# Moving 32 of 128 rows of each value tile from TensorE to GpSimd and VectorE, with wider matmuls around them

## The chip, the core and the metric

The kernel runs on one core of one Trainium2 chip. The metric is the device time of one execution in microseconds, lower is better. Each time is the median of several runs. The profile is one execution on the same chip, recorded by the hardware; its span goes from the first to the last instruction.

## The reference

One decode step for 4 sequences with one token each: a modulation from `c`, attention with 32 heads over a cache of 4096 positions, and a feed-forward block. All in float32.

```
x = A_x                                              # [4, 1, 512]
mod = (silu(c) @ w_mod).reshape(4, 6, 1, 512)        # w_mod [512, 3072]
sa, ca, ga, sb, cb, gb = mod[:, 0], ..., mod[:, 5]
h = layernorm(x) * (1 + ca) + sa
q = (h @ wq).reshape(4, 1, 32, 128).transpose(0, 2, 1, 3)
scores = einsum("bhqd,bhkd->bhqk", q, k_cache) * 128 ** -0.5   # k_cache, v_cache [4, 32, 4096, 128]
o = einsum("bhqk,bhkd->bhqd", softmax(scores), v_cache)
x = x + ga * (o.transpose(0, 2, 1, 3).reshape(4, 1, 4096) @ wo)
h = layernorm(x) * (1 + cb) + sb
x = x + gb * (silu(h @ w1) @ w2)                     # w1 [512, 1792], w2 [1792, 512]
```

The caches are 537 MB of the 567 MB that are read.

## The kernel before

**Tiles.** The work on the caches is cut into N = 32 steps, n = 4t + b: four heads (t = 0 to 7) of one sequence (b = 0 to 3). A step's keys are one tile `k` of 128 partitions x 128 rows x 128 elements, 8.39 MB; partition p holds 128 successive positions of head p // 32 of the four. The values `v` are laid out alike. Three slots of this size (pool `kv`) hold in turn wm, wq, k(0), v(0), k(1), v(1), ... and last the weights wo, and w1 with w2. SP issues all their loads (`fetch`, L82), in order, each when the tile before it in its slot has been read for the last time: k(n+1) goes where v(n-1) was, v(n+1) where k(n) was, wo where v(30) was, w1 and w2 where k(31) was.

**A step.** `make_qb` spreads the query of the step's four heads over the partitions by a matmul (`qb` in PSUM) and copies it to SBUF (`qw`). `mult` multiplies the keys by it in place (L252): GpSimd the first NA = 56 rows, VectorE the other 72. `red` (L257, VectorE) sums each row to a score in `sc` [128, 128]: first the 72 rows, later the 56. `rowmax`, `bmax` (a transpose on TensorE) and `negmax` make the head's maximum; `softexp` takes the exponential (ScalarE), and then GpSimd spreads the result into `pz`, two block-diagonal operands for TensorE, each for half of the rows. `pv` (L297) then multiplies with the values: 32 matmuls, each with 32 columns of `pz` and four value rows (512 elements), spread over four groups of TensorE's columns, and summed in PSUM (`po`) over two steps.

**Every two steps** `gather` picks from `po` what belongs together (VectorE, L308) and adds it by four matmuls into `od` (L314); every four steps `norm` and `spread` divide by the sums and turn the result into the operand `oz`.

**The end.** Step 31 loads and multiplies its keys in two halves, so that its first half can begin earlier; of each half GpSimd takes 28 rows, VectorE 36. After the last `pv` come `project` (L346, with wo, for t = 0 to 3, then 4 to 6, then 7), the last `gather` and `spread` between them, the residual (L415), the second layernorm, and the feed-forward block: up (L424), SiLU by tanh (L166 and L167, ScalarE and VectorE), a transpose (L170), down (L434), the last residual (L438, L439) and the output DMAs. `busy` issues matmuls with no use for their result.

**Order.** The schedule is written out by hand: every engine executes its instructions in the order of the program's text, and waits come from the data and the buffers alone. So the order in the loop body is the order on each engine:

Of the kernel before, what the change touches and what calls it, by code (L numbers as in the profile page):

```python
# [17 lines left out]
def kernel(  # L18
# [32 lines left out]
    NA = 56  # L51
    SCALE = 1.0 / math.sqrt(Dh)
# [54 lines left out]
    tmp = s0.take(P)  # L107
    csT, hT = s0.take(NK, W), s0.take(NK, W)
# [50 lines left out]
    for t in pz:  # L159
        nc.gpsimd.memset(t, 0.0)  # L160
    oz = const.tile([P, NT, R, B], F32, name="oz")
# [15 lines left out]
    def mods(dsts, i):  # L177
        p = psum([P, 4, P], "q", 2)
        for u in range(len(dsts)):
            for k in range(NK):  # L180
                for g in range(G):
                    o = (i + u) * D + g * P
                    nc.tensor.matmul(  # L183
                        p[W * g : W * (g + 1), u, :], csT[:, k, :], wmt[:, k, o : o + P],
                        start=k == 0, stop=k == NK - 1,
                    )
        for u, d in enumerate(dsts):
            nc.scalar.activation(
                d, p[:, u, :], AF.Copy,
                scale=0.25 if i + u == 5 else 0.5, bias=1.0 if i + u in (1, 4) else 0.0,  # L190
            )
# [48 lines left out]
    def make_qb(n):  # L240
        m = work.tile([P, Dh], F32, tag="lnu", name=f"qm{n}", bufs=1)
        nc.scalar.activation(m, qn, AF.Copy, scale=sel[:, n : n + 1])  # L242
        p = psum([P, Dh], "q", 2)
        nc.tensor.matmul(p, blk.rearrange("p i x -> p (i x)"), m, start=True, stop=True)  # L244
        qb[n] = p
        qw[n] = work.tile([P, Dh], F32, tag="qw", name=f"qw{n}")
        nc.scalar.activation(qw[n], p, AF.Copy)  # L247
# [27 lines left out]
    def softexp(n):  # L275
# [4 lines left out]
        for h in range(2):  # L280
            nc.gpsimd.tensor_mul(  # L281
                pz[h][:, : HG * W].rearrange("p (g x) -> p g x", g=HG)[:, :, E:].rearrange("p g (i j) -> p g i j", i=HP),
                sc[n][:, HG * JJ * h : HG * JJ * (h + 1)].rearrange("p (g j) -> p g j", j=JJ)
                .unsqueeze(2).to_broadcast([P, HG, HP, JJ]),
                hm.unsqueeze(1).unsqueeze(3).to_broadcast([P, HG, HP, JJ]),
            )

    def pv(n):
# [4 lines left out]
        for j in range(NG):  # L293
# [7 lines left out]
                start=(a == 0 and j < G), stop=(a == 1 and j >= NG - G),  # L301
# [4 lines left out]
    def gather(t, q):  # L306
# [6 lines left out]
        for j in range(JJ):  # L313
            nc.tensor.matmul(  # L314
                od[t], spick[:, 2 - 2 * q : 2 - 2 * q + P], o[:, j, :],
                start=(q == 0 and j == 0), stop=(q == 1 and j == JJ - 1),
            )
# [21 lines left out]
    accp = psum([P, P], "acc", 1)  # L339
    nc.vector.memset(accp, 0.0)  # L340

    def project(lo, hi):
        for t in range(lo, hi):
            for r in range(R):
                for g in range(G):
                    nc.tensor.matmul(  # L346
                        accp[W * g : W * g + B, :], oz[:, t, r, :], wot[:, t, r, g * P : (g + 1) * P],
                        start=(t == 0 and r == 0), stop=(t == NT - 1 and r == R - 1),
                    )
# [3 lines left out]
    for n in range(N):  # L353
# [29 lines left out]
        red(n, 0, NA if n + 1 < N else NA // 2)  # L383
# [14 lines left out]
        if b == B - 1:  # L398
            norm(t)
        pv(n)  # L400
# [5 lines left out]

    idle = psum([P, P], "q", 2)
# [5 lines left out]
    x1, hg, y = (s2.take(P) for _ in range(3))  # L413
    h2T, hid, th, hidT = s2.take(NK, W), s2.take(FG), s2.take(FG), s2.take(NI, W)
# [53 lines left out]
```

## Time and profile before

| | us |
|---|---|
| time, median of 3 runs | 1323.45 (1323.39 to 1323.84) |
| the profiled execution: time | 1323.81 |
| the profiled execution: span | 1321.9 |
| TensorE busy (matmuls) | 398.0 |
| VectorE busy | 923.3 |
| GpSimd busy | 533.5 |
| ScalarE busy | 44.7 |
| mean granted TensorE clock | 0.636 of full |

In the profile PE is TensorE (PEld its weight loads), DVE VectorE, ACT ScalarE, POOL GpSimd, SP the engine that issues the loads. L252 is line 252 of the kernel. A float32 matmul leaves two records. The timeline's rows have the start and the duration in us, then engine, line, operation, the tiles written and read with partitions x elements, and in brackets how long the engine had been idle before and what released it.

### The profile page before, as it was taken

To read this page: it belongs to the slowest core of one execution; us is meant where nothing else is said; L and a number is where in the kernel's file an instruction comes from. 1 tells how busy PE (TensorE), PEld (TensorE's weight loads), DVE (VectorE), ACT (ScalarE), POOL (GpSimd) and SP (SyncE) were. 2 spreads that over 40 slices of the span, in tenths; PEclk is the share of its full clock that TensorE was granted. 3 is DMA by queue.
4 is the path that set the end of the run, shared out by engine and by line. 5 is a ranking of instruction groups with operands and counts; after the bars stand their busy time and mean duration, and the time that the engine had idled before them with its cause. 6 is when DMAs were issued, how large, how long until landed. Compare 5 with 4: busy or idle time off the path is not lost.

```text
span 1321.9 us, 7059 instructions
## 1 busy us (share of the span) xinstructions
PE 398.0 (30%) x2998; PEld 145.4 (11%) x2998; DVE 923.3 (70%) x335; ACT 44.7 (3%) x146; POOL 533.5 (40%) x111
## 2 busy tenths in 40 slices
PE   3321223323123333212333321323332132333146
PEld 2100001101010010101001010100100010010014
DVE  1267877766887666788667678776668876676971
ACT  1100000000000000000000000000000000000000
POOL 1234455433445533354543334454334445433540
PEclk9765566665566666566666656666655666665569
DMA  9999999999999999999999999999999999999998
GB/s 414 441 418 439 442 419 438 439 424 431 441 430 429 437 436 427 436 436 429 435 433 435 428 435 438 426 435 440 423 435 444 418 437 444 419 437 439 420 422 330
DMA packets 12287, 567.76 MB, mean 430 GB/s; under 512 B 1440, under 2 KB 1504, under 8 KB 2272
## 3 DMA queue, kind: packets, MB, share of 16 engines
q1 hardware_dynamic: 12048, 567.29, 99.4%
q8 instruction: 23, 0.38, 0.1%
q14 instruction: 8, 0.07, 0.0%
q0 software_dynamic: 128, 0.01, 0.0%
q10 hardware_dynamic: 80, 0.02, 0.0%
HBM read 567.30 MB, written 0.01 MB: 429 GB/s over the span
## 4 chain that ended last, share of the span: by engine, by line
DMA 32%; issue 31%; POOL 25%; PE 7%; DVE 4%; POOLq 0%; SPq 0%; DVEq 0%
DMA k<-in_A_k_cache_dram 26%; POOL k L252 24%; PE po L297 6%; DMA w<-in_B_w_dram 3%; DMA wq<-in_A_wq_dram 3%; DVE sc L257 3%; DVE k L252 1%; POOL pz L281 1%; PE q L221 1%; PE mx L231 0%; POOLq L281 0%; DVE o L308 0%; PE po L434 0%; PE mx L265 0%; SPq L123 0%
## 5 line engine op out<-in xcount | busy, mean ns | idle before, releaser
L252 POOL TENSOR_TENSOR k<-k,qw 128x7168 f32<-128x7168 f32 (+1 forms) x33 | 491.4, 14893 | 290.1 <-DMA k<-in_A_k_cache_dram 264.7
L257 DVE TENSOR_REDUCE sc<-k 128x72 f32<-128x9216 f32 (+2 forms) x66 | 554.4, 8422 | 1.1
L252 DVE TENSOR_TENSOR k<-k,q 128x9216 f32<-128x9216 f32 (+1 forms) x33 | 312.3, 9463 | 309.3 <-DMA k<-in_A_k_cache_dram 300.1
L297 PE MATMUL po<-v,pz 128*32 128x512 f32 x2048 | 292.1, 735 | 48.6 <-POOL pz L281 47.9
L281 POOL TENSOR_TENSOR pz<-sc,hm 128x256 f32<-128x256 f32 x64 | 37.9, 612 | 458.1 <-ACT sc L279 445.7
L265 PE MATMUL mx<-ident,rm 128*128 128x128 f32 x32 | 14.5, 453 | 531.2 <-DVE rm L261 531.2
L314 PE MATMUL od<-o,spick 128*128 128x128 f32 x128 | 32.3, 431 | 293.4 <-DVE o L308 293.4
L297 PEld LDWEIGHTS po<-v,pz 128*32 128x32 f32 x2048 | 71.2, 132 | 248.2 <-issue 191.9
L265 PEld LDWEIGHTS mx<-ident,rm 128*128 128x128 f32 x32 | 5.8, 181 | 538.8 <-issue 332.1
L314 PEld LDWEIGHTS od<-o,spick 128*128 128x128 f32 x128 | 27.7, 319 | 296.5 <-DVE o L308 296.3
L279 ACT ACTIVATE sc<-sc,nm 128x128 f32<-128x128 f32 x32 | 12.8, 401 | 891.9 <-DVE nm L273 891.9
L270 DVE TENSOR_REDUCE hx<-mx 128x4 f32<-128x128 f32 x32 | 9.3, 291 | 19.7 <-PE mx L265 19.7
L247 ACT ACTIVATE qw<-q 128x128 f32<-128x128 f32 x32 | 8.9, 277 | 302.9 <-PE q L244 302.9
L308 DVE TENSOR_TENSOR o<-po,jm 128x512 f32<-128x512 f32 x16 | 10.9, 680 | 8.4 <-PE po L297 8.4
L244 PE MATMUL q<-qm,blk 128*128 128x128 f32 x64 | 15.6, 326 | 1.5 <-ACT qm L242 1.5
L183 PE MATMUL q<-wm 128*32 128x128 f32 x192 | 9.2, 375 | 20.3 <-DVE wm L170 20.3
L244 PEld LDWEIGHTS q<-qm,blk 128*128 128x128 f32 x64 | 9.5, 188 | 27.0 <-issue 25.1
L242 ACT ACTIVATE qm<-qn,sel 128x128 f32<-128x128 f32 x32 | 12.4, 387 | 0.9 <-DMA xg<-in_A_x_dram 0.9
L221 PE MATMUL q<-wq,wm 128*32 128x512 f32 x64 | 9.3, 748 | 7.4 <-DMA wq<-in_A_wq_dram 7.4
L183 PEld LDWEIGHTS q<-wm 128*32 128x32 f32 x192 | 7.8, 153 | 21.0 <-DVE wm L170 20.3
L261 DVE TENSOR_REDUCE rm<-sc 128x1 f32<-128x128 f32 x32 | 9.1, 284 | 0.9
L167 DVE SCALAR_TENSOR_TENSOR wm<-wm 128x128 f32<-128x128 f32 x1 | 0.3, 291 | 12.3 <-ACT wm L166 12.3
(79 smaller groups left out, 104.2 us busy)
## 6 DMA issues: line engine op xcount, KB each, us to landing
k<-in_A_k_cache_dram SPq DMA_DIRECT2D x2, 4096.0 KB
wm<-in_w_mod_dram SPq DMA_DIRECT2D x1, 6144.0 KB
wo<-in_A_wo_dram SPq DMA_DIRECT2D x1, 4096.0 KB
wo<-in_A_wo_dram SPq DMA_DIRECT2D x1, 2048.0 KB
wo<-in_A_wo_dram SPq DMA_DIRECT2D x2, 1024.0 KB, 35.2
w<-in_B_w_dram SPq DMA_DIRECT2D x2, 1024.0 KB
w<-in_B_w_dram SPq DMA_DIRECT2D x1, 1792.0 KB
w<-in_B_w_dram SPq DMA_DIRECT2D x2, 896.0 KB
```

The lines of the kernel that those rows point to most:

```text
L183: nc.tensor.matmul(p[W * g : W * (g + 1), u, :], csT[:, k, :], wmt[:, k, o : o + P], start=k == 0, stop=k == NK - 1,)
L221: nc.tensor.matmul(pq[i][W * g : W * (g + 1), :], hT[:, k, :], wqt[:, k, ch * CW : (ch + 1) * CW], start=k == 0, stop=k == NK - 1,)
L242: nc.scalar.activation(m, qn, AF.Copy, scale=sel[:, n : n + 1])
L244: nc.tensor.matmul(p, blk.rearrange("p i x -> p (i x)"), m, start=True, stop=True)
L252: eng.tensor_mul(kt[n][:, lo:hi, :], kt[n][:, lo:hi, :], src[n].unsqueeze(1).to_broadcast([P, hi - lo, Dh]))
L257: nc.vector.tensor_reduce(sc[n][:, lo:hi], kt[n][:, lo:hi, :], axis=AX.X, op=ALU.add)
L265: nc.tensor.transpose(p, nm[n].to_broadcast([P, P]), ident)
L279: nc.scalar.activation(sc[n], sc[n], AF.Exp, bias=nm[n], accum_out=rs[t][:, b : b + 1])
L281: nc.gpsimd.tensor_mul(pz[h][:, : HG * W].rearrange("p (g x) -> p g x", g=HG)[:, :, E:].rearrange("p g (i j) -> p g i j", i=HP), sc[n][:, ...
L297: nc.tensor.matmul(po[t, q][W * g : W * (g + 1), :], pz[h][:, o : o + W], vt[n][:, JJ * j : JJ * (j + 1), :].rearrange("p j d -> p (j d)") ...
L308: nc.vector.tensor_mul(o, po[t, q].rearrange("p (j d) -> p j d", j=JJ), jm.unsqueeze(2).to_broadcast([P, JJ, Dh]))
L314: nc.tensor.matmul(od[t], spick[:, 2 - 2 * q : 2 - 2 * q + P], o[:, j, :], start=(q == 0 and j == 0), stop=(q == 1 and j == JJ - 1),)
```

## The change

- `vmult` (new): after `pz`, GpSimd multiplies the first NV = 32 rows of v(n) in place by their weights, for all steps but the last. `first(n)` is 8 (NV // JJ) there, and 0 in the last step.
- `vsum` (new): in the next step, behind VectorE's product with k(n+1) and ahead of its reductions, VectorE sums these 32 rows (the 32 elements of one sum lie 128 elements apart), and one matmul with `hs` adds the sum to `po`.
- `pv` leaves these rows out: 24 matmuls for 32; `pz` has half as many elements for the first operand.
- In the last step GpSimd takes 36 of each half's 64 rows (NL = 72) for 28, VectorE 28 for 36. Both of GpSimd's halves are reduced last.
- `make_qb` makes the queries of four steps with one 512-wide matmul.
- `gather`: VectorE first adds the four parts (a strided reduction), one matmul for four.
- `project`: 512-wide matmuls, a quarter as many; the parts then stand in four groups of partitions and are added by the matmuls `xa` from a copy `ac`.
- `mods`: 512-wide matmuls too, then four products and matmuls to bring the parts in place.
- A tanh on one column, ahead of the feed-forward block.

```diff
+    NL = 72
+    NV = 32
...
+    hs = const.tile([P, W + E], F32, name="hs")
+    nc.vector.memset(hs, 0.0)
+    nc.vector.tensor_copy(hs[:, E : 2 * E].rearrange("p (i j) -> p i j", i=HP)[:, :, 0], hm)
...
     def mods(dsts, i):
...
+        for k in range(NK):
+            for u in range(n):
+                nc.tensor.matmul(
+                    p[W * u : W * (u + 1), :], csT[:, k, :], wmt[:, k, (i + u) * D : (i + u + 1) * D],
+                    start=k == 0, stop=k == NK - 1,
+                )
...
+        for g in range(G):
+            m = mm[:r, g % 2, :n, :]
+            nc.vector.tensor_mul(
+                m, p[:r, g * P : (g + 1) * P].unsqueeze(1).to_broadcast([r, n, P]),
+                hm[:r, :n].unsqueeze(2).to_broadcast([r, n, P]),
+            )
+            nc.tensor.matmul(z[W * g : W * (g + 1), :, :], sel[:r, :], m, start=True, stop=True)
...
     def make_qb(n):
-        m = work.tile([P, Dh], F32, tag="lnu", name=f"qm{n}", bufs=1)
-        nc.scalar.activation(m, qn, AF.Copy, scale=sel[:, n : n + 1])
-        p = psum([P, Dh], "q", 2)
-        nc.tensor.matmul(p, blk.rearrange("p i x -> p (i x)"), m, start=True, stop=True)
-        qb[n] = p
+        if n % B == 0:
+            m = work.tile([P, B, Dh], F32, tag="o", name=f"qm{n}", bufs=1)
+            for b in range(B):
+                nc.scalar.activation(m[:, b, :], qn, AF.Copy, scale=sel[:, n + b : n + b + 1])
+            p = psum([P, B, Dh], "q", 2)
+            nc.tensor.matmul(p, blk.rearrange("p i x -> p (i x)"), m, start=True, stop=True)
+            for b in range(B):
+                qb[n + b] = p[:, b, :]
...
+    def first(n):
+        return NV // JJ if n < N - 1 else 0
+
+    def vmult(n):
+        if first(n):
+            nc.gpsimd.tensor_mul(
+                vt[n][:, :NV, :], vt[n][:, :NV, :], sc[n][:, :NV].unsqueeze(2).to_broadcast([P, NV, Dh])
+            )
+
+    def vsum(n):
+        t, b = divmod(n, B)
+        q, a = divmod(b, 2)
+        s = work.tile([P, Dh], F32, tag="lnu", name="vs", bufs=1)
+        nc.vector.tensor_reduce(s, vt[n][:, :NV, :].rearrange("p j d -> p d j"), axis=AX.X, op=ALU.add)
+        o = (1 - a) * E
+        nc.tensor.matmul(po[t, q][0:W, 0:Dh], hs[:, o : o + W], s, start=False, stop=a == 1)
+
     def pv(n):
...
-        for j in range(NG):
+        f = first(n)
+        for j in range(f, NG):
...
     def gather(t, q):
...
-        for j in range(JJ):
-            nc.tensor.matmul(
-                od[t], spick[:, 2 - 2 * q : 2 - 2 * q + P], o[:, j, :],
-                start=(q == 0 and j == 0), stop=(q == 1 and j == JJ - 1),
-            )
+        s = work.tile([P, Dh], F32, tag="lnu", name="s", bufs=1)
+        nc.vector.tensor_reduce(s, o.rearrange("p j d -> p d j"), axis=AX.X, op=ALU.add)
+        nc.tensor.matmul(od[t], spick[:, 2 - 2 * q : 2 - 2 * q + P], s, start=q == 0, stop=q == 1)
...
             for r in range(R):
-                for g in range(G):
-                    nc.tensor.matmul(
-                        accp[W * g : W * g + B, :], oz[:, t, r, :], wot[:, t, r, g * P : (g + 1) * P],
-                        start=(t == 0 and r == 0), stop=(t == NT - 1 and r == R - 1),
-                    )
+                nc.tensor.matmul(
+                    accp[W * r : W * r + B, :], oz[:, t, r, :], wot[:, t, r, :],
+                    start=t == 0, stop=t == NT - 1,
+                )
...
             mult(nc.vector, qb, n, NA, NJ)
             make_qb(n + 1)
+            if n:
+                vsum(n - 1)
             red(n, NA, NJ)
         else:
             for lo in (0, NJ // 2):
-                mid, hi = lo + NA // 2, lo + NJ // 2
+                mid, hi = lo + NL // 2, lo + NJ // 2
                 mult(nc.gpsimd, qw, n, lo, mid)
                 mult(nc.vector, qb, n, mid, hi)
+                if lo == 0:
+                    vsum(n - 1)
                 red(n, mid, hi)
-            red(n, NJ // 2, NJ // 2 + NA // 2)
...
-        red(n, 0, NA if n + 1 < N else NA // 2)
+        if n + 1 < N:
+            red(n, 0, NA)
+        else:
+            for lo in (0, NJ // 2):
+                red(n, lo, lo + NL // 2)
...
+        vmult(n)
         pv(n)
...
-    nc.vector.tensor_mul(x1, ga, accp)
+    ac = work.tile([P, D], F32, tag="o", name="ac", bufs=1)
+    nc.vector.tensor_copy(ac[:, : D // 2], accp[:, : D // 2])
+    nc.scalar.activation(ac[:, D // 2 :], accp[:, D // 2 :], AF.Copy)
+    xa = psum([P, P], "mx", 2)
+    for g in range(G):
+        nc.tensor.matmul(xa[W * g : W * (g + 1), :], sel, ac[:, g * P : (g + 1) * P], start=True, stop=True)
+    nc.vector.tensor_mul(x1, ga, xa)
     nc.vector.tensor_add(x1, x1, xg)
     busy(4)
     layernorm_mod(hg, x1, sb, cb1)
+    nc.scalar.activation(th[:, 0:1], x1[:, 0:1], AF.Tanh)
```

How this moves instructions, at two places. First VectorE in step 30, a step with a `gather`, before (`k_2222` are its keys):

```order
L252 TENSOR_TENSOR k_2222<-k_2222,q 128x9216
L257 TENSOR_REDUCE sc_2284<-k_2222 128x72
L308 TENSOR_TENSOR o<-po,jm 128x512
L257 TENSOR_REDUCE sc_2284<-k_2222 128x56
L261 TENSOR_REDUCE rm_2302<-sc_2284 128x1
```

and after (`k_1974` the same keys, `v_1946` the values of step 29):

```order
L269 TENSOR_TENSOR k_1974<-k_1974,q 128x9216
L320 TENSOR_REDUCE vs<-v_1946 128x128
L274 TENSOR_REDUCE sc_2028<-k_1974 128x72
L345 TENSOR_TENSOR o<-po,jm 128x512
L351 TENSOR_REDUCE s<-o 128x128
L274 TENSOR_REDUCE sc_2028<-k_1974 128x56
L278 TENSOR_REDUCE rm_2044<-sc_2028 128x1
```

The sum over the values of the step before now stands between the product and all reductions, and a reduction behind `gather`'s product.

Second, the last step. On VectorE before (`k_2281` are its keys):

```order
L252 TENSOR_TENSOR k_2281<-k_2281,q 128x4608
L257 TENSOR_REDUCE sc_2354<-k_2281 128x36
L252 TENSOR_TENSOR k_2281<-k_2281,q 128x4608
L257 TENSOR_REDUCE sc_2354<-k_2281 128x36
L257 TENSOR_REDUCE sc_2354<-k_2281 128x28 x2
L261 TENSOR_REDUCE rm_2363<-sc_2354 128x1
```

and after (`k_2025` the same keys, `v_1998` the values of step 30):

```order
L269 TENSOR_TENSOR k_2025<-k_2025,q 128x3584
L320 TENSOR_REDUCE vs<-v_1998 128x128
L274 TENSOR_REDUCE sc_2089<-k_2025 128x28
L269 TENSOR_TENSOR k_2025<-k_2025,q 128x3584
L274 TENSOR_REDUCE sc_2089<-k_2025 128x28
L274 TENSOR_REDUCE sc_2089<-k_2025 128x36 x2
L278 TENSOR_REDUCE rm_2101<-sc_2089 128x1
```

Four of the last step's reductions and products now stand behind the sum over v(30). On GpSimd, from `pz` of step 30 on, before:

```order
L281 TENSOR_TENSOR pz_118<-sc_2284,hm 128x16x16
L281 TENSOR_TENSOR pz_119<-sc_2284,hm 128x16x16
L252 TENSOR_TENSOR k_2281<-k_2281,qw_2291 128x3584 x2
L281 TENSOR_TENSOR pz_118<-sc_2354,hm 128x16x16
L281 TENSOR_TENSOR pz_119<-sc_2354,hm 128x16x16
```

and after:

```order
L300 TENSOR_TENSOR pz_118<-sc_2028,hm 128x8x16
L300 TENSOR_TENSOR pz_119<-sc_2028,hm 128x16x16
L312 TENSOR_TENSOR v_1998<-v_1998,sc_2028 128x4096
L269 TENSOR_TENSOR k_2025<-k_2025,qw_2031 128x4608 x2
L300 TENSOR_TENSOR pz_118<-sc_2089,hm 128x16x16
L300 TENSOR_TENSOR pz_119<-sc_2089,hm 128x16x16
```

The product with v(30) has come ahead of the two products with k(31), which are larger by 8 rows each.

More of the change, by code (lines that the diff above doesn't have):

```diff
@@ L107 @@
     tmp = s0.take(P)
+    mm = s0.take(2, 4, P)
     csT, hT = s0.take(NK, W), s0.take(NK, W)
@@ L300, in pv @@
                 vt[n][:, JJ * j : JJ * (j + 1), :].rearrange("p j d -> p (j d)"),
-                start=(a == 0 and j < G), stop=(a == 1 and j >= NG - G),
+                start=(a == 0 and j < f + G), stop=(a == 1 and j >= NG - G and (g > 0 or not f)),
             )
@@ L337, in spread @@
         nc.vector.tensor_copy(oz[:, t], ot[:, :, :B])
-    accp = psum([P, P], "acc", 1)
+    accp = psum([P, D], "acc", 1)
     nc.vector.memset(accp, 0.0)
@@ L405 @@
     project(NT - 1, NT)
+    x1, hg, y = (s2.take(P) for _ in range(3))
+    h2T, hid, th, hidT = s2.take(NK, W), s2.take(FG), s2.take(FG), s2.take(NI, W)
     idle = psum([P, P], "q", 2)
```

29 lines of the change are left out of this document (12 added, 17 removed).

## The prediction

> **What bounds the kernel now.** I read the page first (busy shares, slices), then the timeline of some loop iterations and of the last 70 us, then the groups with shapes kept apart.
>
> ```profile
> span 1321.9 us, 7059 instructions
> PE 398.0 (30%) x2998; PEld 145.4 (11%) x2998; DVE 923.3 (70%) x335; ACT 44.7 (3%) x146; POOL 533.5 (40%) x111
> DMA  9999999999999999999999999999999999999998
> GB/s 414 441 418 439 442 419 438 439 424 431 441 430 429 437 436 427 436 436 429 435 433 435 428 435 438 426 435 440 423 435 444 418 437 444 419 437 439 420 422 330
> ```
>
> No engine is full, but the DMA engines are, in every slice: 567 MB at about 432 GB/s. PE, from which the change takes work, is busy 30%. So the loop goes as fast as key and value tiles arrive, and computing matters in two ways only: whether it frees a buffer in time for the next transfer, and how long it runs on after the last bytes. Here is an iteration (n = 10) in the timeline; column one is the start in us, column two the duration.
>
> ```profile
> 445.30 9.75 DVE L252 TENSOR_TENSOR k<-k,q 128x9216 f32<-128x9216 f32 x1 [10.07 <-DMA k<-in_A_k_cache_dram]
> 446.52 0.33 SPq L82 DMA_DIRECT2D k<-in_A_k_cache_dram  x1
> ...
> 465.35 7.61 DVE L257 TENSOR_REDUCE sc<-k 128x56 f32<-128x7168 f32 x1
> 472.99 0.33 SPq L82 DMA_DIRECT2D v<-in_A_v_cache_dram  x1
> 475.20 1.19 POOL L281 TENSOR_TENSOR pz<-sc,hm 128x256 f32<-128x256 f32 x2 [14.56 <-ACT sc L279]
> 475.87 9.04 PE L297 MATMUL po<-v,pz 128*32 128x512 f32 x64 [1.99 <-POOL pz L281]
> 484.05 9.75 DVE L252 TENSOR_TENSOR k<-k,q 128x9216 f32<-128x9216 f32 x1 [9.46 <-DMA k<-in_A_k_cache_dram]
> ...
> 523.67 9.76 DVE L252 TENSOR_TENSOR k<-k,q 128x9216 f32<-128x9216 f32 x1 [9.16 <-ACT qw L247]
> ...
> 553.49 0.16 DVE L273 TENSOR_REDUCE nm<-hx 128x1 f32<-128x4 f32 x1
> ```
>
> Call T the moment key tile n has landed (445.3, then 484.0: a period of 38.8 us, 19.4 for each 8.39 MB tile). With three slots, the load of k(n+1) waits until v(n-1) is consumed: issued at T+1.2, needed moving by T+19.4. The load of v(n+1) waits until k(n) is reduced: issued at T+27.7, needed moving by T+38.8. From issue to the first bytes is about 1 us:
>
> ```profile
> 0.74 0.40 SPq L123 DMA_DIRECT2D wm<-in_w_mod_dram  x1
> ...
> 0.00:1.00 1.00, 0.00 (x0) 0.00 (x0) 0.16 (x2) 0.00 (x0) 0.47 (x6) 1.00 0.00 0
> 1.00:2.00 1.00, 0.00 (x0) 0.00 (x0) 0.01 (x2) 0.00 (x0) 0.76 (x2) 1.00 1.90 590
> ```
>
> (the last number is GB/s). Taking a few tenths more for the completion signal, a k load must be issued by about T+18, a v load by about T+37.4: reserves of 17 and 10 us today.
>
> **The prices.** Groups with shapes kept apart; the last numbers before the second bar are busy us and mean ns of one.
>
> ```profile
> L252 POOL TENSOR_TENSOR k<-k,qw 128x7168 f32<-128x7168 f32 x31 | 475.8, 15350 | 290.1 <-DMA k<-in_A_k_cache_dram 264.7 <-PE po L297 16.8 <-PE q L244 8.6
> L252 POOL TENSOR_TENSOR k<-k,qw 128x3584 f32<-128x3584 f32 x2 | 15.6, 7816 | 0.0
> L281 POOL TENSOR_TENSOR pz<-sc,hm 128x256 f32<-128x256 f32 x64 | 37.9, 612 | 458.1 <-ACT sc L279 445.7 <-issue 12.4
> L257 DVE TENSOR_REDUCE sc<-k 128x36 f32<-128x4608 f32 x2 | 9.9, 4953 | 0.1
> L257 DVE TENSOR_REDUCE sc<-k 128x28 f32<-128x3584 f32 x2 | 7.7, 3876 | 0.0
> L140 DVE TENSOR_REDUCE hm<-ident 128x4 f32<-128x128 f32 x1 | 0.3, 279 | 0.0
> L144 DVE TENSOR_REDUCE jm<-ident 128x4 f32<-128x128 f32 x1 | 0.4, 368 | 0.0
> L135 DVE TENSOR_REDUCE sel<-ident 128x32 f32<-128x128 f32 x1 | 0.4, 376 | 3.2 <-POOL ident masks.py:199 3.2
> ```
>
> GpSimd's product over 32 value rows (`vmult`, 4096 elements), call it V: slope (15350-7816)/3584 = 2.10 ns, fixed 0.28, so V = 8.9 us. Its second operand is constant along 128 elements, which only pz resembles: 612 ns for 256 less 0.28 is 1.30 ns each, so 5.6 as the low end; 612/256 = 2.39 each, so 9.8 as the high. I take 8.9, the form nearest in size and layout.
>
> VectorE's sum over these rows (`vsum`), call it S: with contiguous reads 3.876 + 512 x 1.05 = 4.41 us. But it reads down the rows, with a stride of 512 bytes. L140 and L144 reduce the same 128 elements, L140 contiguously (279 ns), L144 with a stride of 16 bytes (368): 0.695 ns more an element, so S = 4.41 + 2.85 = 7.26. L135, stride 128 bytes, gives 0.76 more, so 7.5. I take 7.26, a reduction like it, and keep 4.41 and 7.5 as ends. The reduction that `gather` gains (512 elements) is 1.04 likewise.
> The Trainium skill, SBUF — State Buffer, section "Door 1: The DMA port swizzle", says that SBUF has 16-byte lines and that an access that moves to a new line pays; L144 against L140 agrees, with 0.09 us on 128 elements. The skill's VectorE: DVE Perf Modes, section "Walkthrough: the 8-slice pipeline in each mode", has the 1x mode handle fp32 and odd strides at one element a cycle; by that S would be an estimated 4.4 us, and the sum the second rival's below.
>
> **The change in the loop.** On DVE `vsum(n-1)` stands behind the product with k(n), so k(n+1) is issued not at T+1.2 but at T+9.75+7.26 = T+17.0: 1 us of reserve left. That load, and the v load behind it on SP, wait for it. Reductions end 7.26 later, in a gather iteration 8.3: v(n+1) issued at T+36.0 instead of T+27.7, 1.4 us of reserve. pz starts at T+38.2, takes about 1.0 (half of one operand gone), and V ends at T+48.1, which is 9.3 into the next period; DVE needs it at 9.75. GpSimd's next product then ends at 24.7, needed at 26.8. DVE's fullest iteration (523.67 to 553.65, 30.0 us) becomes 38.3 of 38.8. PE loses 8 of 32 matmuls, some 2 us of the 9.04, and gains one small matmul; nothing waits there. So all of it just fits, and the loop costs 0: the cover is the transfer of the tile ahead, and each us beyond the reserve of the k load would cost some 30 us in all.
>
> A gain in the loop is excluded, since the transfers set its pace and stay as they are.
>
> ```profile
> 38.38 9.33 PE L221 MATMUL q<-wq,wm 128*32 128x512 f32 x64 [7.36 <-DMA wq<-in_A_wq_dram]
> ...
> 57.81 9.75 DVE L252 TENSOR_TENSOR k<-k,q 128x9216 f32<-128x9216 f32 x1 [30.58 <-DMA k<-in_A_k_cache_dram]
> ```
>
> Start of the kernel: modulation gains four DVE products and four dependent matmuls a call, some 3 us a call by my estimate, but PE then stands idle 7.4 us for wq, and DVE 30.6 for k(0): 0. The query broadcast made for four heads at once takes matmuls from an idle PE: 0, with the same cover.
>
> **The change at the end.** Here nothing covers.
>
> ```profile
> 1252.21 1.18 POOL L281 TENSOR_TENSOR pz<-sc,hm 128x256 f32<-128x256 f32 x2 [14.54 <-ACT sc L279]
> 1253.35 15.59 POOL L252 TENSOR_TENSOR k<-k,qw 128x3584 f32<-128x3584 f32 x2
> 1266.39 12.54 DVE L257 TENSOR_REDUCE sc<-k 128x36 f32<-128x4608 f32 x3
> 1281.97 8.77 PE L297 MATMUL po<-v,pz 128*32 128x512 f32 x64 [0.16 <-POOL pz L281]
> 1290.56 3.67 PE L346 MATMUL acc<-wo,oz 128*4 128x128 f32 x128
> 1294.16 1.16 PE L314 MATMUL od<-o,spick 128*128 128x128 f32 x8
> 1300.46 1.06 PE L346 MATMUL acc<-wo,oz 128*4 128x128 f32 x32 [1.48 <-DMA wo<-in_A_wo_dram]
> 1301.58 0.29 DVE L415 TENSOR_TENSOR w<-mod,acc 128x128 f32<-128x128 f32 x1 [5.32 <-PE acc L346]
> 1305.50 2.46 PE L424 MATMUL q<-w 128*32 128x448 f32 x24 [0.15 <-DVE w L170]
> 1310.10 1.28 ACT L166 ACT_TABLE_LOAD   x1 [5.67 <-PE q L424]
> 1311.39 0.54 ACT L166 ACTIVATE w<-q 128x448 f32<-128x448 f32 x1
> 1313.62 1.95 PE L434 MATMUL po<-w 128*32 128x128 f32 x64 [2.09 <-DVE w L170]
> 1317.81 0.43 PE L434 MATMUL po<-w 128*32 128x128 f32 x8 [0.21 <-DMA w<-in_B_w_dram]
> 1318.62 0.29 DVE L439 TENSOR_TENSOR w<-w 128x128 f32<-128x128 f32 x1
> ```
>
> Before, the reductions of the last key tile end at 1266.39+12.54 = 1278.9, and the rest of the chain waits three times for weights (1300.46, and twice more to 1317.81): it has slack.
>
> After: pz(30) starts 8.3 later, 1260.5, ends 1261.5; `vmult(30)` runs to 1270.4. DVE has done its first product with k(31) by 1264 and stands in `vsum(30)` until then: 1270.4+7.26 = 1277.7. Behind it in order: three pieces of 28 rows at 3.88 (1289.3) and two reductions of 36 rows at 4.95: 1299.3, that is 20.3 late. GpSimd's own halves (10.0 each) end at 1280.4 and 1290.4, in time.
> From there to the start of pv is 3.0, then 8.77 (the last tile keeps all its rows): 1311.1. `project(0,4)` streams as many columns in fewer matmuls, 3.67: 1314.8; gather's product and reduction lie beside it. `od` 0.3; `project(4,8)` 3.67, spread beside it: 1318.8, no weight to wait for. New: copies of acc, about 0.4, and the four `xa` matmuls, about 0.5: x1 starts at 1319.7, 18.1 late. To the first FFN matmul 3.9: 1323.6. FFN up without its waits: 32 records at the 0.1 of the 24 (2.46): 3.2; tanh 0.65 with its table loaded earlier (1.28 saved); product and transpose as before, 1.6 to 1.7: 1329.1. Down: 112 records at 1.95/64 = 30.5 ns, 3.4: 1332.5. The last DVE product ends 0.6 later, 1333.1, where it was 1318.9: **14.2 us later**. Between 20.3 and 14.2 lie the old waits for weights and the table load. The weights themselves are no bound: the w1 and w2 load (7.34 MB) is issued at 1299.3, as wo is ending, and at 420 GB/s is in by about 1319, ahead of its use.
>
> Profiled run 1323.81 (span 1321.9 and 1.9 around it), 0.36 above the median of 1323.45. The sum gives 1338.0 on that run; on the median, 1337.7.
>
> **Rivals.**
> 1. *The stride is dearer than that, and the loop leaves its cover* (slower still). From S = 8.2 the k load is late, in each of 30 periods. If a strided element cost twice a contiguous one (2.1 ns), S = 8.7: 0.5 x 30 = 15, and 2 x 1.4 at the end: about 1355. For it: 1 us of reserve. Against: both strided rows stand under 7.6.
> 2. *The stride is free*: S = 4.41, reductions of the last tile end 2 x 2.85 + 0.36 = 6.1 earlier: 1331.6. Against: L144. With V = 5.6 as well, 1328.3, the low end.
> 3. *Not slower: GpSimd's product with a value constant along the row is so short that DVE never waits for it.* The old slack absorbs 6.1 of the 20.3 us, the measurable bound of 0.2% (2.65 us) 2.65 more. With S = 4.41 this needs V under 3.4 us, 0.75 ns an element, where no GpSimd product here goes under 1.3. It then gives about 1324; well below 1323 it cannot go, since w2's last piece lands at 1317.8 either way.
>
> **From this to the numbers.** My sum 0.70, rival 1 0.12, rival 2 (with its low end) 0.11, rival 3 0.07. The forecast is 1337.7. The range, 1328 to 1350, takes in both ends of S and V and the near part of rival 1 (S up to 8.5); outside lie rival 3 and the far part of rival 1. Faster by over 0.2% (what a measurement of this kernel can tell): 0.03; within 0.2%: 0.05; slower: 0.92.
>
> **What would show it.** After: a `vs` group on DVE at 7.0 to 7.5 us; a GpSimd group of 4096 elements at 8.9; a period still of 38.8 us, its k load issued about T+17; in the last iteration DVE idle some 6 us before `vs`, released by POOL; last reduction at about 1299; no wait for weights in the FFN. Wrong if `vs` is near 4.4, if the period grows, or if the end is not where the time goes.

## The result, and the profile after

The changed kernel takes 1372.02 us (median of 6 runs, 1369.16 to 1376.03), the kernel before 1323.74 beside it: 1.0369 times as long (95% interval 1.0348 to 1.0389), 48.3 us slower. That is the forecast sign and 34 us more than the forecast, above its range. The profiled execution is the slowest of the six, 1376.03, so its parts below add up to some 3 us more than 48.3. First the page of after: its span and instructions, the busy times, and the DMA throughput in the 40 slices.

```profile
span 1373.5 us, 5429 instructions
PE 344.2 (25%) x2108; PEld 100.0 (7%) x2108; DVE 1158.1 (84%) x393; ACT 45.2 (3%) x148; POOL 747.0 (54%) x142
GB/s 418 436 428 415 412 418 403 428 422 421 408 401 409 416 426 411 416 424 403 418 432 424 407 418 428 414 418 426 428 401 408 414 430 426 428 429 420 405 413 230
```

TensorE lost 54 us of work and VectorE gained 235, GpSimd 214, none of which is full. What fell is the throughput, in the whole loop: between the first slices and the last one they read 401 to 432, where they read 418 to 444 before. The transfers set the pace, and fewer bytes arrive in each microsecond.

Where the time lies is read from T(30), the start of VectorE's product with k(30), in the timelines of before (first row) and after:

```profile
1222.31 9.76 DVE L252 TENSOR_TENSOR k<-k,q 128x9216 f32<-128x9216 f32 x1 [10.46 <-DMA k<-in_A_k_cache_dram]
```

```profile
58.18 9.76 DVE L269 TENSOR_TENSOR k<-k,q 128x9216 f32<-128x9216 f32 x1 [20.40 <-DMA k<-in_A_k_cache_dram]
...
1262.09 9.76 DVE L269 TENSOR_TENSOR k<-k,q 128x9216 f32<-128x9216 f32 x1 [4.80 <-DMA k<-in_A_k_cache_dram]
...
1300.95 7.04 POOL L312 TENSOR_TENSOR v<-v,sc 128x4096 f32<-128x4096 f32 x1
...
1308.02 7.14 DVE L320 TENSOR_REDUCE vs<-v 128x128 f32<-128x4096 f32 x1 [4.86 <-POOL v L312]
...
1322.78 13.61 DVE L274 TENSOR_REDUCE sc<-k 128x28 f32<-128x3584 f32 x3
...
1361.04 3.21 PE L473 MATMUL q<-w 128*32 128x448 f32 x32 [0.15 <-DVE w L176]
...
1366.61 3.27 PE L483 MATMUL po<-w 128*32 128x128 f32 x112 [0.82 <-DVE w L176]
...
1370.26 0.29 DVE L488 TENSOR_TENSOR w<-w 128x128 f32<-128x128 f32 x1
```

T(30) came 39.8 us later. With T(0) at 57.81 before and 58.18 after, a period is 38.82 us before and 40.13 after: 1.3 us more, 30 times. The rest of the span, from T(30) on, is 99.6 us before (1321.9 - 1222.31) and 111.4 after: 11.8 more. So nearly four fifths of the loss lie in the loop, where the prediction had put nothing.

One step of the loop after (n = 9), in the timeline:

```profile
418.27 0.97 POOL L300 TENSOR_TENSOR pz<-sc,hm 128x128 f32<-128x128 f32 x2 [20.29 <-ACT sc L296]
...
419.19 7.03 POOL L312 TENSOR_TENSOR v<-v,sc 128x4096 f32<-128x4096 f32 x1
...
420.53 9.75 DVE L269 TENSOR_TENSOR k<-k,q 128x9216 f32<-128x9216 f32 x1 [2.93 <-DMA k<-in_A_k_cache_dram]
...
430.20 7.12 DVE L320 TENSOR_REDUCE vs<-v 128x128 f32<-128x4096 f32 x1
...
437.38 0.33 SPq L84 DMA_DIRECT2D k<-in_A_k_cache_dram  x1
...
454.53 0.33 SPq L84 DMA_DIRECT2D v<-in_A_v_cache_dram  x1
...
461.50 9.76 DVE L269 TENSOR_TENSOR k<-k,q 128x9216 f32<-128x9216 f32 x1 [5.42 <-DMA k<-in_A_k_cache_dram]
```

VectorE is not the pace: it stands idle 5.42 us before the next product, waiting for keys. GpSimd's product is done at 426.2, 4 us before the sum wants it. The k load is issued at T+16.9, as forecast, and the next T is 41.0 later. What happens around that issue is in the stretches of 1 us (the last two columns are the busy share of the DMA engines and GB/s, both booked where a packet begins, so that a share can pass 1), after:

```profile
435.00:436.00 1.00, 0.00 (x0) 0.00 (x0) 1.00 (x1) 0.00 (x0) 1.00 (x1) 0.50 0.45 197
436.00:437.00 1.00, 0.00 (x0) 0.00 (x0) 1.00 (x1) 0.00 (x0) 1.00 (x1) 0.50 0.31 131
437.00:438.00 1.00, 0.63 (x2) 0.18 (x2) 1.00 (x2) 0.00 (x0) 1.00 (x1) 0.50 0.16 66
438.00:439.00 1.00, 0.01 (x1) 0.00 (x0) 1.00 (x1) 0.00 (x0) 1.00 (x1) 0.50 2.71 918
439.00:440.00 1.00, 0.00 (x0) 0.00 (x0) 1.00 (x1) 0.00 (x0) 1.00 (x1) 0.50 0.15 66
```

and the same place in a step of before (v(10) ends, k(11) begins):

```profile
462.00:463.00 1.00, 0.00 (x0) 0.00 (x0) 1.00 (x1) 0.00 (x0) 0.00 (x0) 0.50 0.61 262
463.00:464.00 1.00, 0.00 (x0) 0.00 (x0) 1.00 (x1) 0.00 (x0) 0.00 (x0) 0.50 1.37 590
464.00:465.00 1.00, 0.00 (x0) 0.00 (x0) 1.00 (x2) 0.00 (x0) 0.00 (x0) 0.50 0.91 393
465.00:466.00 1.00, 0.51 (x2) 0.51 (x3) 1.00 (x2) 0.00 (x0) 0.00 (x0) 0.50 1.06 459
466.00:467.00 1.00, 1.00 (x7) 1.00 (x6) 1.00 (x1) 0.00 (x0) 0.00 (x0) 0.50 1.06 459
```

A packet is one partition's row, 8.39 MB / 128 = 65.5 KB, so 66 GB/s in a microsecond is one packet that begins. Each of the 16 DMA engines carries 8 of a tile's 128 packets. Before, 6.6 begin in a microsecond on average, 4 to 9 in the rows shown. After, from 435 to 438, 6 begin where 20 would have; then 14 at once between 438 and 439, about 1 us after the issue at 437.38. The engines do not finish a tile together: by the packet records they run out one by one, here from 436.97 to 439.53, and the load issued at 437.38 finds 10 of the 16 already idle.

### The profile page after: what moved, and what is told of

Read it like the earlier page. It is cut to its first block, busy times and chain, and to the rows that moved or that the text cites. A ratio compares the mean times of both kernels' runs of the same rounds, so it can differ in the third digit from the quotient of the medians.

```text
span 1373.5 us, 5429 instructions
## 1 busy us (share of the span) xinstructions
PE 344.2 (25%) x2108; PEld 100.0 (7%) x2108; DVE 1158.1 (84%) x393; ACT 45.2 (3%) x148; POOL 747.0 (54%) x142
## 4 chain that ended last, share of the span: by engine, by line
DMA 47%; issue 25%; DVE 18%; POOL 6%; PE 4%; ACT 0%; ACTq 0%; SPq 0%; DVEq 0%; POOLq 0%
DMA k<-in_A_k_cache_dram 46%; DVE vs L320 14%; POOL k L269 5%; DVE sc L274 3%; DMA wm<-in_c_dram 1%; PE po L334 1%; PE q L188 1%; POOL v L312 1%; PE q L235 1%; PE acc L380 1%; PE q L200 0%; PE po L483 0%; PE q L473 0%; POOL pz L300 0%; DVE wm L196 0%
## 5 line engine op out<-in xcount | busy, mean ns | idle before, releaser
L300 POOL TENSOR_TENSOR pz<-sc,hm 128x128 f32<-128x128 f32 (+1 forms) x64 | 31.2, 509 | 537.0 <-ACT sc L296 537.0
L334 PE MATMUL po<-v,pz 128*32 128x512 f32 x1552 | 241.6, 788 | 44.1 <-POOL pz L300 44.0
L320 DVE TENSOR_REDUCE vs<-v 128x128 f32<-128x4096 f32 x31 | 220.8, 7123 | 4.9 <-POOL v L312 4.9
L312 POOL TENSOR_TENSOR v<-v,sc 128x4096 f32<-128x4096 f32 x31 | 218.1, 7035 | 0.0
L322 PE MATMUL po<-vs,hs 128*32 128x128 f32 x62 | 19.7, 421 | 361.2 <-DVE vs L320 361.2
L334 PEld LDWEIGHTS po<-v,pz 128*32 128x32 f32 x1552 | 56.7, 140 | 207.2 <-issue 155.8
L352 PE MATMUL od<-s,spick 128*128 128x128 f32 x32 | 12.2, 484 | 160.8 <-DVE s L351 160.8
L352 PEld LDWEIGHTS od<-s,spick 128*128 128x128 f32 x32 | 7.8, 304 | 168.2 <-DVE s L351 89.0
L351 DVE TENSOR_REDUCE s<-o 128x128 f32<-128x512 f32 x16 | 16.3, 1021 | 0.6
L188 PE MATMUL q<-wm 128*32 128x512 f32 x48 | 9.9, 714 | 20.4 <-DVE wm L176 20.4
```

Of the source, the lines that this page charges most:

```text
L188: nc.tensor.matmul(p[W * u : W * (u + 1), :], csT[:, k, :], wmt[:, k, (i + u) * D : (i + u + 1) * D], start=k == 0, stop=k == NK - 1,)
L300: nc.gpsimd.tensor_mul(pz[h][:, f * W : HG * W].rearrange("p (g x) -> p g x", g=m)[:, :, E:].rearrange("p g (i j) -> p g i j", i=HP), sc[n ...
L312: nc.gpsimd.tensor_mul(vt[n][:, :NV, :], vt[n][:, :NV, :], sc[n][:, :NV].unsqueeze(2).to_broadcast([P, NV, Dh]))
L320: nc.vector.tensor_reduce(s, vt[n][:, :NV, :].rearrange("p j d -> p d j"), axis=AX.X, op=ALU.add)
L322: nc.tensor.matmul(po[t, q][0:W, 0:Dh], hs[:, o : o + W], s, start=False, stop=a == 1)
L334: nc.tensor.matmul(po[t, q][W * g : W * (g + 1), :], pz[h][:, o : o + W], vt[n][:, JJ * j : JJ * (j + 1), :].rearrange("p j d -> p (j d)") ...
```

## The experiments

**Theory A**: the k load, held back to T+16.9 by the sum, comes too late for DMA engines that run dry from about T+16 on; only its issue time matters. **Rival B**: the added work itself (GpSimd's product in the landing tiles' memory, the strided sum) slows the transfers. **Rival C**: something else, such as other parts of the change. (In the expectations of kernels 1 and 2, "theory C" is a narrower one: VectorE is too full, so that the load of the values comes late.) The first four kernels are set beside 1323.88 us for the kernel before. Kernels 1, 2, 5, 7, 8, 10 and 11 are single runs, the others 4 to 11; the six runs of the changed kernel spread over 6.9 us.

**1. The sum between two halves of VectorE's product.**

```
-            mult(nc.vector, qb, n, NA, NJ)
-            make_qb(n + 1)
+            mult(nc.vector, qb, n, NA, NA + 36)
             if n:
                 vsum(n - 1)
+            mult(nc.vector, qb, n, NA + 36, NJ)
+            make_qb(n + 1)
```

> The changed kernel with one move: VectorE's product with k(n+1) is cut in two halves of 36 rows, and the sum over the 32 value rows stands between them. Work and traffic stay the same; the load of the next key tile should be issued some 4 us earlier, at about T+12.8 (T: key tile landed; the sum then waits for GpSimd's product, to T+5.7 at most) instead of T+16.9. Theory A (late load: the DMA engines finish the value tile from T+16.5 on, so a load issued at T+16.9 finds most of them idle and pays for a restart): the period falls from 40.1 to 38.8-39.0 us, the time to 1332-1338 us, with only the longer end left. Theory B (the added work on GpSimd and the strided reads on VectorE slow the transfers themselves, whenever the load is issued): period 40, time 1368-1376. Theory C (VectorE is too full, so that the load of the value tile, issued at T+35.7 in a gather step, comes late): no better than 1365, since VectorE's work has not shrunk.

It took 1386.41 us, slower still. The expectation missed what the timeline shows (n = 14, with T = 619.69):

```profile
618.23 0.33 SPq L84 DMA_DIRECT2D v<-in_A_v_cache_dram  x1
...
619.69 4.96 DVE L269 TENSOR_TENSOR k<-k,q 128x4608 f32<-128x4608 f32 x1
...
628.43 7.18 DVE L320 TENSOR_REDUCE vs<-v 128x128 f32<-128x4096 f32 x1 [3.78 <-POOL v L312]
...
635.67 0.33 SPq L84 DMA_DIRECT2D k<-in_A_k_cache_dram  x1
```

The sum now comes up 3.8 us before GpSimd's product ends, and VectorE waits 89 us in all for it. Its step grows by as much, so that the v load goes out 1.5 us before the next T and has become the late one: by the landing times 1.7 us are lost on each, and the period is 40.39. It did not tell A from B; it showed that VectorE has no room for a wait. That is the narrower theory C, here made true by the move; in the changed kernel itself a v load loses 0.15 us and a k load 1.33 (the table below tells how this is counted).

**2. No sum** (`vsum` left out in every step, `vmult` kept).

```
-                start=(a == 0 and j < f + G), stop=(a == 1 and j >= NG - G and (g > 0 or not f)),
+                start=(a == 0 and j < f + G), stop=(a == 1 and j >= NG - G),
...
-            if n:
-                vsum(n - 1)
...
-                if lo == 0:
-                    vsum(n - 1)
```

> The changed kernel without VectorE's sum over the 32 value rows and its matmul (these rows are left out of the result); GpSimd still multiplies them, TensorE still leaves them out. Theory A: the key load then waits for GpSimd's product alone, T+5.7 at most, so the period is 38.8; at the end GpSimd's halves come 8 us late and most of that meets the old waits for weights: 1323-1328 us. Theory B, if GpSimd's product is what slows the transfers: still above 1345; if it is the strided reads: as A. Theory C: as A.

1323.88 us, the time of before, period 38.78. GpSimd's product in place, 7.04 us in each step, slows no transfer and lengthens nothing. Half of B is gone.

**3. 16 rows** (`NV = 16`).

```
-    NV = 32
+    NV = 16
```

> The changed kernel with 16 value rows for 32 (NV = 16). Sum about 3.6 us, product about 3.6, key load issued at about T+13.4. Theory A: a threshold, not a slope: the period is back at 38.8; at the end the last reduction comes 7 to 8 us late instead of 18, of which the old waits take 6: 1323-1328 us. Theory B: about half the loss, 1345-1350 us.

1325.1 us (1324.37 to 1326.2), 1.0010 times before (1.0001 to 1.0019): half of the rows cost 1.2 us, not half of 48. The k load is issued at T+13.4, the period is 38.78. A threshold lies between T+13.4 and T+16.9.

**4. The rest of the change alone** (no rows moved, 28 rows of each half for GpSimd in step 31; modulation, queries, `gather`, `project` and the early tanh as changed).

```
-    NL = 72
-    NV = 32
+    NL = 56
+    NV = 0
...
-            if n:
-                vsum(n - 1)
...
-                if lo == 0:
-                    vsum(n - 1)
```

> The other parts of the change alone: no value rows leave TensorE (NV = 0), and GpSimd has 28 rows of each half in the last step as before (NL = 56); modulation, query, gather, project and the early tanh as changed. All theories: 1323-1325 us, since the transfers set the pace and the last weights land when they did; the gather's reduction adds 1 us to VectorE every second step, which is hidden.

1324.46 us, 1.0005 (0.9995 to 1.0015): nothing measurable. Rival C's best candidate is out.

**5. The kernel before, with its k load held by other work.** This kernel and the next three are set beside 1323.78 us for the kernel before.

```
+    extra = const.tile([P, 52], F32, name="extra")
...
             make_qb(n + 1)
+            if n:
+                nc.vector.tensor_reduce(extra[:, :52], vt[n - 1][:, NJ - 52 :, :], axis=AX.X, op=ALU.add)
             red(n, NA, NJ)
```

> The kernel before, with one thing added: behind VectorE's product with k(n), in steps 1 to 30, a reduction with contiguous reads of 52 rows of v(n-1) into a tile that nobody reads (52 x 128 elements, 7.1 us by the reductions of before). It holds the load of k(n+1) back to about T+16.9, as in the changed kernel, but there is no GpSimd work on the values and no strided read, and the end is the old one. Theory A (the late k load lets the DMA queue run dry, since most of the 16 engines finish tile v(n) from T+16.5 on): the period grows to 40.0 to 40.4 us and the time to 1360 to 1372 us. Rival B (GpSimd's product and the strided sum disturb the transfers that land meanwhile): period 38.8, time 1323.5 to 1325. Rival C (the load issued at T+17 is in time, as predicted, and the loss is in something else): the same 1323.5 to 1325.

1364.84 us. The timeline, two starts of the product with the k load between them:

```profile
1220.99 9.76 DVE L252 TENSOR_TENSOR k<-k,q 128x9216 f32<-128x9216 f32 x1 [2.10 <-DMA k<-in_A_k_cache_dram]
...
1237.80 0.33 SPq L82 DMA_DIRECT2D k<-in_A_k_cache_dram  x1
...
1260.84 9.75 DVE L252 TENSOR_TENSOR k<-k,q 128x9216 f32<-128x9216 f32 x1 [4.36 <-DMA k<-in_A_k_cache_dram]
```

Issue at T+16.8, mean period 40.09. The loop's whole loss is there without one instruction of the change. A holds; B and C give 1324.

**6. All the work, without the hold.** In steps 1 to 30 the sum reads keys instead of values.

```
-                vsum(n - 1)
+                vsum(n - 1, kt[n][:, NJ - NV :, :])
```

> The changed kernel, but in steps 1 to 30 the strided sum reads 32 rows of k(n) in place of v(n-1) (it sums the wrong rows; shape, stride, engine and place in the order are the same; the last step keeps the true sum). So all the work of the change is done, but k(n+1) waits only for GpSimd's product over v(n-1) and the matmuls, which are done by about T+9, not for the sum at T+17. Theory A: period 38.8, the loop's 40 us are gone and only the end's 10 to 14 us stay: 1333 to 1338 us. Rival B (contention of the added work with the transfers): unchanged, 1366 to 1376 us.

1349.86 us (1348.33 to 1351.79), 1.0198 (1.0181 to 1.0215). Neither number: 22 us of the loss went, and 12 to 17 more remain than A had said. From the timeline:

```profile
606.85 9.76 DVE L269 TENSOR_TENSOR k<-k,q 128x9216 f32<-128x9216 f32 x1 [3.86 <-DMA k<-in_A_k_cache_dram]
...
612.31 0.33 SPq L84 DMA_DIRECT2D k<-in_A_k_cache_dram  x1
...
642.65 0.33 SPq L84 DMA_DIRECT2D v<-in_A_v_cache_dram  x1
...
645.90 9.75 DVE L269 TENSOR_TENSOR k<-k,q 128x9216 f32<-128x9216 f32 x1 [1.64 <-DMA k<-in_A_k_cache_dram]
```

The k load is now early (T+5.5), but in a step with a `gather` the v load goes out at T+35.8, 3.2 us before the next T: the same lateness, on the other load. In the landing times every second v tile, the one loaded in a step with a `gather`, loses 0.9 us, the others 0.1; the 30 v loads together make 15.6 us, and v(30) lands 14.9 later than in the kernel before. In the changed kernel the k tile's own delay moves the next T out and so hides most of this. That reading was tested in 9 and 10.

**7. A shorter hold**: as 5, with 40 rows for 52.

> As the kernel with 52 added contiguous rows, with 40 rows (5.4 us): the k load is held to about T+15.3, 1.6 us earlier, still behind nothing else. Theory A with its threshold at the time when the first DMA engines run dry (T+16.5, less about 1 us from issue to first packets): just at it, the period 38.8 to 38.9, 1324 to 1327 us; and if the loss were in proportion to the delay rather than past a threshold, 5.4/7.1 of the loss of the kernel with 52 rows, some 1350 to 1358 us. Rivals B and C: 1323.5 to 1325.

1342.16 us: neither the few microseconds of a sharp threshold at T+15.5 nor the 1350 of proportion.

```profile
1200.84 9.76 DVE L252 TENSOR_TENSOR k<-k,q 128x9216 f32<-128x9216 f32 x1 [3.66 <-DMA k<-in_A_k_cache_dram]
...
1216.06 0.33 SPq L82 DMA_DIRECT2D k<-in_A_k_cache_dram  x1
...
1239.92 9.75 DVE L252 TENSOR_TENSOR k<-k,q 128x9216 f32<-128x9216 f32 x1 [5.17 <-DMA k<-in_A_k_cache_dram]
```

At T+15.2, mean period 39.39, 0.6 us is lost each time. The loss begins earlier than A had put it, and grows as a ramp.

**8. The old end**: the changed kernel with steps 30 and 31 as before.

```
-    NL = 72
+    NL = 56
...
-        return NV // JJ if n < N - 1 else 0
+        return NV // JJ if n < N - 2 else 0
...
-                if lo == 0:
-                    vsum(n - 1)
```

> The changed kernel, but steps 30 and 31 work as before (no product and sum over v(30), and GpSimd takes 28 rows of each half in step 31): the loop is the changed one up to step 29, the end that of before. By the reading of the two traces, in which the span grows 51.6 us, 39.8 of them before step 30 and 11.8 behind it: 1372 less 10 to 12, so 1358 to 1363 us. If the loop's loss came from the end (it does not by the traces), 1324.

1364.39 us, just above the expected 1358 to 1363. From T(30) at 1260.31 to the end of the span it is 102.3 us: 9.1 less than after, 2.7 more than before. Kernel 5, with the old end, late k loads and nothing of the change, has 102.2, so these 2.7 come with the late k loads.

**9. Both loads cut in two.** All the work of the change in the same order; the two loads of a step go out as soon as their rows are free. This kernel and the next two are set beside 1323.69 us for the kernel before.

```
-            load_k(n + 1)
+            load_k(n + 1, NV, NJ)
...
                 vsum(n - 1)
+                if n < N - 2:
+                    rest(kt, kc, n + 1, 0, NV)
...
             red(n, NA, NJ)
+            load_v(n + 1, NA, NJ)
...
-            load_v(n + 1)
+            rest(vt, vc, n + 1, 0, NA)
```

(`rest` loads rows lo to hi of a tile; the three slots are fixed buffers there, so that waits go by rows. The load of k(31) is still issued behind the sum, as in the changed kernel, and that of wo behind the last sum.)

> The changed kernel with all its work, in the same order on every engine, computing the reference; only the loads are cut in two. Rows 32 to 127 of k(n+1) are loaded when TensorE has done with v(n-1) (about T+7), rows 0 to 31 when the sum has (T+17); rows 56 to 127 of v(n+1) when VectorE has reduced them in k(n) (T+27), rows 0 to 55 at T+35 to T+36. The DMA queue then always has at least 7 MB of 8.4 ahead when the late piece is issued. Theory A (the loss is a queue that runs dry because a load is issued too late): period 38.8 to 38.9 us, the end as in the changed kernel (111 us from T(30) on, 12 more than before): 1333 to 1338 us. Rival B (the added work slows the transfers, part of the loss when the sum read keys instead of values): 1345 to 1376 us.

1334.93 us (1333.96 to 1335.47), 1.0082 (1.0065 to 1.0099), inside A's 1333 to 1338. From T(1) to T(30) a period is 38.9 us. The changed kernel with nothing taken away but the lateness of its loads (that of k(31) apart) loses 11 us instead of 48. In its trace v(30) lands 4.4 us later than in the kernel before, so some 4 of the 11 still lie ahead of the end, and 7 in it.

**10. Only the k load cut.**

> As the kernel with both loads cut, but v(n+1) is loaded in one piece again, at T+36 in a step with a gather. Theory A, from the run in which the sum read keys: the k load is early and the v load late by itself, 0.55 us lost a period, 39.2 to 39.3 us and 1346 to 1352 us. Rival B: the same as the kernel with both loads cut, wherever that is, within 2 us.

1332.03 us, where A's number was 1346 to 1352. The timeline at step 30 shows what was overlooked:

```profile
1218.19 9.76 DVE L277 TENSOR_TENSOR kv<-kv,q 128x9216 f32<-128x9216 f32 x1 [3.22 <-DMA kv<-in_A_k_cache_dram]
...
1223.99 15.37 POOL L277 TENSOR_TENSOR kv<-kv,qw 128x7168 f32<-128x7168 f32 x1 [0.39 <-DMA kv<-in_A_k_cache_dram]
```

VectorE needs rows 56 to 127 alone, which are all in the first piece, and starts 5.8 us ahead of GpSimd, which waits for the second piece. Everything on VectorE, the v load behind it included, moves as far ahead of the transfers, so the v load is no longer late in one piece either: it goes out 6.1 us or more before the mean landing of the piece ahead. Rival B's number, that of kernel 9 within 2 us, was missed too, by 0.9. By this the two kernels agree with A, but 10 does not isolate the v load as it was meant to; that the v load made the rest of 6 rests on its issue and landing times.

**11. 24 rows** (`NV = 24`).

> The changed kernel with NV = 24 rows for 32: sum and product 5.3 us each, the k load at about T+15.2, between the 13.5 of NV = 16 (1325.1) and the 17.0 of NV = 32 (1372.0). Theory A, from the kernel with 40 added rows, whose k load is issued at the same time (18 us lost): 1323.9 + 18 and 4 to 8 us at the end: 1342 to 1352 us. Were the loss in proportion to the rows moved: 1360.

1341.75 us, just under the 1342 to 1352 of A. The k load goes out at T+15.1; the loop loses 10 us (period 39.15) and the end 7.4 (107.0 from T(30)). With 16, 24 and 32 rows the whole costs 1.2, 18 and 48 us.

**12. The k load cut, and the old end**: 10 with the edits of 8.

> The kernel with only the k loads cut in two (1332.0), with steps 30 and 31 as before the change (no product and sum over v(30), 28 rows of each half for GpSimd), computing the reference: all of the change's work in steps 0 to 29, but neither the late load nor the longer end. If the loss of the changed kernel (48.3 us) is the late k load (loop) and the longer end and nothing else, this is within 3 us of the kernel before: 1322 to 1327 us. If something of the added work still costs, 1328 or more. It cannot come out more than a us or two under the kernel before, whose transfers stand close together up to the last weights.

1325.78 us (1325.62 to 1325.98) against 1323.85, 1.0014 (1.0005 to 1.0023). The 48.3 us are accounted for to within 2: with the rows moved in steps 0 to 29 as the change has it, but loads issued in time and the old end, hardly anything is lost. No version came out under the kernel before.

## Why the prediction was wrong, point by point

- **The step that failed is "a k load must be issued by about T+18, a v load by about T+37.4", and with it "1 us of reserve left" and "the loop costs 0".** It counted back from the moment the tile ahead has landed, which is the end of its last engine, while the others run dry up to 3 us earlier. The 1.4 us that it had from the issue to the flow of bytes (1 us from the start of the kernel, and a few tenths for which it showed no row) were not far off: in after the first packets of most k loads begin 0.96 us behind the issue, and an engine's landing stands 0.4 us behind its last packet.
  The traces of after and of kernels 1, 3, 5, 6, 7, 8 and 11 give the true price. A tile lands in 16 parts, one per DMA engine; I take the mean of the 16 landing times of the tile ahead, less the issue time, as the lead, and what the next tile takes beyond 19.36 us (8 packets of 2.42), from mean to mean, as the loss. Of k(2) to k(30) and v(1) to v(30) (8 more loads, issued behind the mean landing, lost 2.35 on average):

| lead, us | loads | mean loss, us |
|---|---|---|
| 0 to 1 | 48 | 1.71 |
| 1 to 2 | 58 | 1.19 |
| 2 to 3 | 59 | 0.57 |
| 3 to 4 | 78 | 0.19 |
| 4 to 5 | 103 | 0.06 |

  Kernels 5 and 7, which have nothing of the change but a held k load, lose as much at the same lead (1.74, 1.35, 0.63, 0.20, 0.13) as the kernels with added work (1.70, 1.14, 0.54, 0.18, 0.04), which leaves nothing for rival B. The k loads of after have a mean lead of 1.27 us and a mean loss of 1.33; this is the period's growth. To lose next to nothing takes 4 us of lead. The mean landing of v(n) lies at T+18.1 (the issue at T+16.86 and the lead of 1.27), so the bound is T+14.1 and not T+18: NV = 16 (T+13.4, lead 4.6, loss 0.01) is inside, T+15.2 outside, T+16.9 far outside. For the v load, with the mean landing of k(n+1) some 1.6 us ahead of the next T (kernel 6), the same count gives T+33.2 and not T+37.4, and a step with a `gather` issues it at T+35.7.
  The Trainium skill, DMA: Bandwidth & Descriptors, section "Anatomy of one DMA — SWDGE (gpsimd) path", gives each DMA a fixed cost of about 2.0 us, most of it the confirmation that the last byte has landed. Its figure is for DMAs issued by GpSimd; for these, issued by SP, the packet records show the 0.96 and 0.4 us just named, no more than 0.4 of it behind the last packet. With 2.0 in place of my 1.4 us the deadline would be an estimated T+17.4, which the issue at T+16.9 still meets; the 4 us are not in it.
  Nor are engines that run dry early all of it. In after the first of the 16 landings of v(n) comes at T+17.5 on average, and 1.4 us ahead of that is T+16.1; yet kernels 7 and 11, at T+15.2 and T+15.1, lose 0.6 and 0.4 us a load. By the packet records an engine stands idle 1.11, 0.56, 0.19 and 0.04 us at the switch of tiles in the first four rows of the table, and its packets there take 0.67, 0.72, 0.52 and 0.35 us more than 2.42 each would make, enough for the rest. So in the step of kernel 7 shown above, issued at 1216.06: the first engine ends its last packet of the values at 1218.32 and begins one of the keys at once, and this one takes 2.78. Why such packets are longer stays open.
- **Rival 1 named the right event ("the loop leaves its cover") with the wrong cause and threshold.** It needed S above 8.2. S was 7.12 as forecast; by the bound of T+14.1 the cover ends at about S = 4.4, between 3.67 (NV = 16) and 5.40 (NV = 24). Nor does each microsecond of lateness cost 30 us in all: from 40 to 52 added rows, 1.6 us later, it was 22.7 us, 14 for each. Rivals 2 and 3 are out: S was not 4.41, and V, 7.04, not under 3.4.
- **S and V.** The groups of after, mean ns of one behind the first bar:

```profile
L320 DVE TENSOR_REDUCE vs<-v 128x128 f32<-128x4096 f32 x31 | 220.8, 7123 | 4.9 <-POOL v L312 4.9
L312 POOL TENSOR_TENSOR v<-v,sc 128x4096 f32<-128x4096 f32 x31 | 218.1, 7035 | 0.0
...
L351 DVE TENSOR_REDUCE s<-o 128x128 f32<-128x512 f32 x16 | 16.3, 1021 | 0.6
```

  S, 7.26 in the sum, measured 7.12, and `gather`'s 1.04 is 1.02: the price of the stride, taken from two setup reductions of 128 elements, holds at 4096 within 0.14 us. The estimate of 4.4 from the Trainium skill's VectorE: DVE Perf Modes, section "Walkthrough: the 8-slice pipeline in each mode", differs from the measurement, and the measurement decides. V, 8.9 in the sum, measured 7.04: mis-sized by 1.9, within its bounds of 5.6 and 9.8.
- **The steps around the loop were right**: k load at T+16.9 (forecast 17.0), pz at T+37.9 (38.2), the v load up to T+35.7 (36.0), VectorE never waiting for GpSimd before step 31. Modulation, queries and the first steps cost nothing (T(0) at 58.18 for 57.81; kernel 4).
- **The end: 14.2 later forecast, 11.8 measured.** The steps came as laid out (five instructions stand behind the sum over v(30), as the forecast counted, and not the four of the section on the change): VectorE idle in the last iteration before the sum, released by POOL, 4.86 us (forecast some 6); last reduction at T(30) + 74.3 (forecast 77.0, before 56.6); no wait for weights; FFN up 3.21 (3.2), down 3.27 (3.4). The last product ends at T(30) + 108.5, where the forecast had 110.8. The step mis-sized is V: 1.9 of the 2.3.
- **Slower** was right in sign for the end's sake alone; had the loop cost as little as in kernel 9, its 1334.93 would have stood 3 us from the forecast, and in part by luck, with 4 us ahead of the end and 7 in it for 0 and 14.

## What to carry to other kernels

Where transfers set the pace, ask of every load how long before the tile ahead has landed it is issued, and take that tile's landing not as one moment but as 16 engines that end one after the other: here 4 us before the mean of them cost next to nothing and 1.3 us cost 1.3 a tile. An instruction that is harmless on a half-idle engine is dear if it is the last reader of the buffer that the next load waits for; moving 16 rows cost 1 us, moving 32 cost 48. When such a reader cannot come earlier, cutting the load at the rows it reads gives back the cover, here for some 2 us in all with 30 more loads.

## What the hardware did that I had not expected

- A late load costs well before the DMA engines have all stopped, and as a ramp: about half a microsecond for each microsecond of lead missing under 3.5. In the DMA records of after the 14 packets that begin together from 438.3 on take 2.7 to 3.5 us, where 19.36 / 8 = 2.42 is the rule: the restart itself is slow too.
- The kernels with late loads scatter more: six runs of after spread over 6.9 us, eleven of kernel 12 over 0.4. Why was not tried.
- GpSimd's product with the values, whose second operand is constant along the row, is cheaper than that with the keys: 7035 ns for 4096 elements and 5323 for 3072, 1.67 ns each, against 2.12 between 15361 ns for 7168 and 9928 for 4608 with keys and query. That the constant operand is the reason was not tried.
- The strided sum costs 1.68 ns an element (7123 ns for 4096, 5402 for 3072), against 1.05 with contiguous reads.
- More and smaller loads seem not quite free: kernel 12, with 30 more DMAs, stays 1.9 us above before, and its v(30) lands 2.0 us later (kernel 10, with the same loads, 1.9; kernel 9, with 60 more, 4.4). In kernels 2, 3 and 4, which do work of the change with whole loads, it lands 0.2 to 0.5 later. No run adds the loads alone.
